# Routing tables, first-slot weights and weight loads re-ordered in an attention and mixture-of-experts kernel

## The chip, the cores and the metric

The kernel runs on one core of one Trainium2 chip. The metric is the device time of one execution in microseconds (us), the median of a few runs. All times inside an execution are counted from the start of the profiled span.

## What is computed

```python
def reference(**kw):
    attn_out = _attn_ref(q, k, v)                 # rotary attention, 4 x 8 heads, 576 x 64
    x = attn_out as rows                          # (2304, 512)
    x = _moe_ref(x, w_gate, w_val, w_out)         # sigmoid(x@wg) * (x@wv) @ wo, d_ff 1536
    return _moe2_ref(x, ...)

def _moe2_ref(x, modality_id, w_gate, modality_bias, w1, w2):   # 2304 tokens, 8 experts
    logits = x @ w_gate + modality_bias[modality_id]
    e_idx = np.argmax(logits, axis=1)
    probs = softmax(logits)
    gate_w = probs[np.arange(N), e_idx]
    for e in range(E):
        mask = e_idx == e
        h = np.maximum(x[mask] @ w1[e], 0.0)      # (512, 1024)
        out[mask] = gate_w[mask, None] * (h @ w2[e])
    return out
```

Only the last part, `_moe2_ref`, and the end of the layer ahead of it are touched here.

## The kernel before

The kernel has three stages: attention (to about 260 us), the gated layer (to about 772 us) and the experts (to the end). Every product of two fp32 operands is made of three TensorE products: each operand is a high part in fp32r and a low part (the rest), and low times low is left out.

The end of the gated layer, `Gated.last`, makes the 18 output blocks of 128 tokens (TensorE L822, then an addition on VectorE, L1115, then a store to the row table `x2_rows` in HBM, L1125, issued from the SP queue) and, beside them, the routing. The order of this stretch is set by `Plan`: it simulates the engines with given costs and, on each engine, takes the ready step with the lowest priority number. Output block tt has priority 1000 + tt, its store 999 + tt, all routing steps -2.

The routing (`Router.route`, L1294) finds each token's expert and its place in that expert's list of slots of 256 tokens. At the end it makes three tables with one matmul chain: for each half slot and row, the token, and the high and low part of its gate weight. The operands are a one-hot of the place (`A`, written into `wb` and `spare`; a part of it is made on ScalarE from `r_d`) and three products of the one-hot of the half slot (`r_B`): with the token number, and with the two gate parts `r_gw`. The products go in three groups of 8, 8 and 2 token blocks. `tables` (L1438) turns the result, `r_ptab`, into the gather indices `r_gi`, the scatter indices `r_si` and the gates.

`Experts` then works through nine full slots and the rest. Per slot: two gathers of 128 rows by index on GpSimd's queue (`e_xg`, L1530), transposes (`e_pt`, L1541), split into `e_xh` and `e_xl`; layer 1 (96 matmuls into `e_ph`, L1560, four buffers' worth of output in three buffers); Relu and split into `e_hh` (ScalarE, L1562) and `e_hl` (VectorE, L1563); layer 2 (48 matmuls into `e_py`, L1578); scaling by the gate (L1592) and a scatter (L1593). A slot's weights come in eight parts of 512 KB: four of w1, four of w2. Each part is loaded into one of six raw buffers `wr` (L1498), copied to a high part on ScalarE (`high`, L1516) and a low part on VectorE (`low`, L1520) into one of twelve weight tiles (`e_wa`, `e_wb`, `e_w`).

The first slot's four w1 parts are loaded from SP as soon as its expert is known. Three of them are split inside the plan, between routing steps; the fourth follows in `Experts.run`. Then come `keep_warm(8)`, eight fp32 matmuls of 512 columns whose result nobody reads (L1470), and the first inputs. The w2 parts of the first slot and two w1 parts of the second are loaded from ScalarE's queue, behind the first inputs; all others from SP, each four parts ahead of its split.

Of the kernel before, what the change touches and what calls it, by code (L numbers as in the profile page):

```python
# [20 lines left out]
KC = 4  # L21
# [620 lines left out]
class Gated:  # L642
# [346 lines left out]
    def last(self, prev, r, experts):  # L989
# [196 lines left out]
class Router:  # L1186
# [107 lines left out]
    def route(self, plan, start, ps_pool, area):  # L1294
# [108 lines left out]
        do("DVE", 0.09, None, tt(out=gw[:, 1], in0=su[:, 1], in1=f32(gw[:, 0]), op=ALU.subtract), "gw")  # L1403
        do("DVE", 0.67, ["pos"], tt(out=Bm, in0=bc(self.c("ioc"), 1, NTT), in1=bc(pos[:, 2], 2, NCOL), op=ALU.is_equal), "Bm")
        groups = ((0, 8), (8, 16), (16, 18))
        for g, (k, e) in enumerate(groups):
            n, s = e - k, slice(k, e)
            A, Bv = (area[4][:, 0:256], area[4][:, 256:448]) if g == 2 else (area[2 * g], area[2 * g + 1][:, 0:768])
            Bv = Bv.rearrange("p (t a c) -> p t a c", t=n, a=3)
# [13 lines left out]
            do("DVE", 0.07 + 0.034 * n, ["Bm"], tt(out=Bv[:, :, 0], in0=Bm[:, s], in1=bc(self.c("tok")[:, s], 2, NCOL), op=ALU.mult))  # L1423
            for j in range(2):
                do("DVE", 0.07 + 0.034 * n, ["gw", "Bm"], tt(out=Bv[:, :, 1 + j], in0=Bm[:, s], in1=bc(f32(gw[:, j, s]), 2, NCOL), op=ALU.mult), f"Bv{g}")

            def table(k=k, n=n, A=A, Bv=Bv):
# [6 lines left out]
            do("PE", 0.11 * n, [f"A{g}", f"Bv{g}"] + [f"table{g - 1}"] * (g > 0), table, f"table{g}")  # L1434
        ids["table"] = ids["table2"]
        plan.add("DVE", 0.1, lambda: self.tables(st["pt"]), [ids["table"]], -2)

    def tables(self, pt):  # L1438
        V = self.nc.vector
        tt = V.tensor_tensor  # L1440
        tab = self.k([128, 4, NCOL], "r_tab")
        V.tensor_scalar(out=tab[:, 0], in0=pt[:, 0:NCOL], scalar1=-1.0, scalar2=None, op0=ALU.add)
        self.gi = self.k([128, NCOL], "r_gi", I32)
        self.si = self.k([128, NCOL], "r_si", I32)
        V.tensor_scalar(out=self.gi, in0=tab[:, 0], scalar1=0.0, scalar2=None, op0=ALU.max)
        V.tensor_scalar(out=tab[:, 1], in0=tab[:, 0], scalar1=0.0, scalar2=BIG, op0=ALU.is_lt, op1=ALU.mult)
        tt(out=self.si, in0=tab[:, 0], in1=tab[:, 1], op=ALU.add)
        V.tensor_copy(tab[:, 2], pt[:, NCOL:2 * NCOL])
        tt(out=tab[:, 3], in0=pt[:, 2 * NCOL:3 * NCOL], in1=tab[:, 2], op=ALU.add)
        self.gate = tab[:, 3]  # L1450


class Experts:
    NW = 12

    def __init__(self, tc, rawpool, xs, router, w1, w2, x2d, out, ident):
        self.tc, self.nc, self.rawpool, self.xs = tc, tc.nc, rawpool, xs
# [7 lines left out]
    def keep_warm(self, n):  # L1465

        cst = self.r.cst
        ps = self.ps.tile([128, 2, SL], F32, name="e_ph", tag="e_ph", bufs=3)
        for _ in range(n):
            self.nc.tensor.matmul(ps.rearrange("p a b -> p (a b)"), self.ident, cst[:, 0:2 * SL], start=True, stop=True)  # L1470

# [6 lines left out]
                self.t(shape, name, dt, n)  # L1478

    def load_reg(self, s):  # L1480
        engines = (mybir.EngineType.SP, mybir.EngineType.Activation)[0:2 if s < 2 else 1]
        return self.nc.values_load(self.r.esi[0:1, s:s + 1], engines=engines, min_val=0, max_val=NE - 1,
                                   skip_runtime_bounds_check_because="clamped on chip")

    def load(self, s, k, dma=None):

        nc = self.nc
        if k == 0:
# [9 lines left out]
        (dma or nc.sync.dma_start)(out=dst, in_=src)  # L1498
        self.raw[s, k] = raw

    def w_tile(self):
# [45 lines left out]
    def layer1(self, s, x, between):  # L1547
# [5 lines left out]
        for f2 in range(4):  # L1553
            ps = self.ps.tile([128, 2, SL], F32, name="e_ph", tag="e_ph", bufs=3)
            for k in range(2):
                f = 2 * f2 + k
                fs = slice(128 * f, 128 * f + 128)
                mm = [(a, c, xh) for c in range(KC) for a in w[c]] + [(w[c][0], c, xl) for c in range(KC)]
                for n, (a, c, b) in enumerate(mm):
                    nc.tensor.matmul(ps[:, k], a[:, fs], b[:, c], start=n == 0, stop=n == 3 * KC - 1)  # L1560
            fs = slice(2 * f2, 2 * f2 + 2)
            nc.scalar.activation(out=hh[:, fs], in_=ps, func=AF.Relu)  # L1562
            nc.vector.scalar_tensor_tensor(out=hl[:, fs], in0=ps, scalar=0.0, in1=f32(hh[:, fs]), op0=ALU.max, op1=ALU.subtract)  # L1563
            between(f2)
        return hh, hl

# [71 lines left out]
    def run(self, pool, psum):  # L1638
# [1 line left out]
        self.pool, self.ps = pool, psum  # L1640
        self.place()
        xg = self.gather(0)
        self.split(0, KC - 1)
        self.keep_warm(8)
        x = self.inputs(0, xg)
        for k in range(KC):
            self.load(0, KC + k, nc.scalar.dma_start)
        for k in range(KC):
            self.split(0, KC + k)
            self.load(1, k, nc.scalar.dma_start if k < 2 else None)  # L1650
        for s in range(NFULL):
            last = s + 1 == NFULL

            def first(k):
                self.split(s + 1, k)
                self.load(s + 1, 4 + k)

            def second(k):
                self.split(s + 1, 4 + k)
                if not last:  # L1660
                    self.load(s + 2, k)
# [98 lines left out]
```

## Time and profile before

| | us |
|---|---|
| median of 3 runs | 1024.36 (1021.84 to 1025.43) |
| the profiled execution | 1025.67 |
| its span, first to last instruction | 1023.9 |
| TensorE busy | 987.3 (96%) |
| VectorE busy | 658.3 (64%) |
| ScalarE busy | 524.0 (51%) |
| mean granted TensorE clock | 0.994 |

The page gives, for each engine, busy time and share of the span. TensorE is busy almost throughout, and matmuls overlap, so its busy share alone does not tell how near its limit it is. The granted clock is a share of full speed: 1.0 is 2.4 GHz, 0.5 is 1.2 GHz. Of a group of overlapping instructions the timeline shows the start of the first, the time to the end of the last and their count; in brackets the idle time ahead of it and what ended it.

### The profile page before, as it was taken

Reading aid. Unit: us, or ns where it says so; the run is one execution under the profiler, and the core shown is the slowest. Engines: PE = TensorE matmul, PEld = TensorE weight load, DVE = VectorE, ACT = ScalarE, POOL = GpSimd, SP = SyncE. Lnnn points to the kernel's source line nnn. Section 1 sums busy time; section 2 is a strip of 40 time slices with the busy share of each in tenths; the row PEclk is TensorE's granted clock in tenths of the full one; section 3 lists DMA queues with packets and bytes.
Section 4 is the critical chain, followed back from the end, with each engine's and each line's share of the span. In section 5 each row is a group of like instructions: output and inputs, shape, how many; then the busy total and the mean of one; then the engine's idle time right before and its main releaser. Section 6 shows DMA issues by size and latency. Waiting matters only on the chain.

```text
span 1023.9 us, 16353 instructions
## 1 busy us (share of the span) xinstructions
PE 987.3 (96%) x6085; PEld 908.6 (89%) x6085; DVE 658.3 (64%) x1196; ACT 524.0 (51%) x1038; POOL 352.1 (34%) x272
## 2 busy tenths in 40 slices
PE   8899999998999999999999999999998899999996
PEld 7889899988989999999999999998886899999994
DVE  8999999999977746535535536422365655556651
ACT  6889899888967422222212222223313555555542
POOL 5888769565313423223313322301101021111111
PEclk9999999999999999999999999999999999999998
DMA  6897777765311302101101101000046966767640
GB/s 209 249 264 186 203 190 197 186 171 148 93 54 62 104 21 64 42 21 62 49 14 62 62 22 43 20 1 1 1 139 223 325 225 221 223 226 225 222 161 25
DMA packets 61399, 128.42 MB, mean 125 GB/s; under 512 B 6575, under 2 KB 20543, under 8 KB 61312
## 3 DMA queue, kind: packets, MB, share of 16 engines
q1 hardware_dynamic: 56896, 114.45, 37.2%
q0 software_dynamic: 3040, 9.70, 2.9%
q10 hardware_dynamic: 1376, 3.15, 0.8%
q8 instruction: 50, 0.82, 0.3%
q14 instruction: 37, 0.30, 0.1%
HBM read 95.65 MB, written 9.77 MB: 103 GB/s over the span
## 4 chain that ended last, share of the span: by engine, by line
PE 51%; issue 18%; ACT 6%; DMA 6%; DVE 6%; POOL 2%; SPq 0%; POOLq 0%; DVEq 0%; ACTq 0%
PE gv L753 29%; PE yo L822 13%; DMA out<-e_y,r_si 5%; PE pv L322 2%; ACT e L244 2%; ACT pth L305 2%; PE s L222 2%; DVE e L232 2%; DVE ptl L309 2%; PE pt L275 1%; PE gv L822 1%; POOL e_xg L1530 1%; PE r_pl L1270 1%; PE r_pt L1234 1%; ACT xv L330 1%
## 5 line engine op out<-in xcount | busy, mean ns | idle before, releaser
L762 POOL TENSOR_TENSOR gl<-sg,gh 128x384 fp32r<-128x384 f32 x60 | 63.4, 1057 | 259.5 <-ACT gh L761 259.5
L760 DVE TENSOR_TENSOR sg<-gv,sg 128x384 f32<-128x384 f32 x70 | 39.0, 557 | 142.1 <-PE gv L753 122.3
L244 ACT ACTIVATE e<-e,st 128x576 f32<-128x576 f32 x144 | 112.1, 782 | 12.7 <-DVE e L232 12.0
L759 ACT ACTIVATE sg<-gv 128x384 f32<-128x384 f32 x70 | 34.4, 491 | 145.1 <-PE gv L753 144.9
L232 DVE TENSOR_SCALAR_CACHE_REDUCE e<-s 128x576 f32<-128x576 f32 x144 | 105.3, 747 | 4.8 <-PE s L222 4.3
L309 DVE TENSOR_TENSOR ptl<-pt,pth 128x512 fp32r<-128x512 f32 x144 | 93.7, 679 | 2.8 <-ACT pth L305 1.7
L1593 POOL DMA_INDIRECT out<-e_y,r_si x19 | 19.6, 1031 | 190.3 <-ACT e_y L1592 190.3
L275 PE MATMUL pt<-cst,e 128*128 128x128 f32 x576 | 79.9, 274 | 5.1 <-DVE ptl L309 3.9
L1520 DVE TENSOR_TENSOR e_w<-wr,e_w 128x1024 fp32r<-128x1024 f32 x59 | 71.1, 1222 | 21.0 <-ACT e_w L1516 19.9
L222 PE MATMUL s<-sb 128*128 128x288 f32 x336 | 76.4, 319 | 6.4 <-DVE e L232 4.0
L761 ACT CAST gh<-sg 128x384 fp32r<-128x384 f32 x60 | 30.8, 514 | 100.4 <-DVE sg L760 100.4
L305 ACT CAST pth<-pt 128x512 fp32r<-128x512 f32 x144 | 79.3, 588 | 5.4 <-PE pt L275 4.2
L322 PE MATMUL pv<-pth,vv 128*128 128x256 f32 (+1 forms) x256 | 73.4, 309 | 6.2 <-DVE xy L340 4.6
L753 PE MATMUL gv<-xe,wb 128*128 128x384 f32 x384 | 78.9, 338 | 0.0
L275 PEld LDWEIGHTS pt<-cst,e 128*128 128x128 f32 x576 | 66.6, 141 | 9.0 <-DVE ptl L309 4.9
L753 PE MATMUL gv<-xh,wb 128*128 128x384 f32 x288 | 74.1, 338 | 0.0
L322 PE MATMUL pv<-ptl,vv 128*128 128x256 f32 (+1 forms) x256 | 69.8, 295 | 0.0
L753 PEld LDWEIGHTS gv<-xe,wb 128*128 128x128 f32 x384 | 67.1, 188 | 1.2
L1578 PE MATMUL e_py<-e_w,e_hh 128*128 128x512 f32 x216 | 67.2, 392 | 0.0
L753 PE MATMUL gv<-xh,wr 128*128 128x384 f32 x288 | 66.7, 335 | 0.0
L753 PE MATMUL gv<-xe,wr 128*128 128x384 f32 x336 | 65.0, 335 | 0.3 <-ACT xe L867 0.3
L753 PE MATMUL gv<-xl,wb 128*128 128x384 f32 x192 | 64.3, 335 | 0.0
(298 smaller groups left out, 2543.9 us busy)
## 6 DMA issues: line engine op xcount, KB each, us to landing
wr<-in_w SPq DMA_DIRECT2D x74, 512.0 KB
sb<-sa SPq DMA_DIRECT2D x60, 288.0 KB
sa<-in_qk SPq DMA_DIRECT2D x18, 576.0 KB
xy<-in_qk SPq DMA_DIRECT2D x12, 576.0 KB
wraw<-in_wg SPq DMA_DIRECT2D x12, 512.0 KB
wraw<-in_wv SPq DMA_DIRECT2D x12, 512.0 KB
wraw<-in_wo SPq DMA_DIRECT2D x12, 512.0 KB
vraw<-in_v SPq DMA_DIRECT2D x16, 320.0 KB
```

The costliest lines, as they stand in the source:

```text
L222: nc.tensor.matmul(ps[:, u, 0:SH], a, m[:, SH * u:SH * u + SH], start=n == 0, stop=n == len(mm) - 1)
L232: self.nc.vector.tensor_scalar(out=e, in0=ps[:, :, 0:SH], scalar1=-0.125, scalar2=3.0e38, op0=ALU.mult, op1=ALU.min, accum_out=st[:, 0])
L244: nc.scalar.activation(out=e, in_=e, func=AF.Exp, bias=st[:, 0], scale=-1.0, accum_out=st[:, 1])
L275: nc.tensor.transpose(pt[:, c], e[:, 128 * c:128 * c + 128], self.ident)
L305: self.nc.scalar.copy(out=hi, in_=src)
L309: self.nc.vector.tensor_tensor(out=lo, in0=src, in1=f32(hi), op=ALU.subtract)
L322: nc.tensor.matmul(ps[:, 0:w], a, m, start=n == 0, stop=n == len(mm) - 1)
L753: self.nc.tensor.matmul(p[:, 0:U], a[:, wc], b[:, c], start=c == 0 and n == 0, stop=c == KC - 1 and n == 2)
L762: (eng, {"POOL": 0.93, "DVE": 0.47}[eng], lambda: low.tensor_tensor(out=gl, in0=sg, in1=f32(gh), op=ALU.subtract))]
L822: nc.tensor.matmul(ps, a, b, start=n == 0, stop=n == 3 * len(GROUPS[grp]) - 1)
L1520: self.nc.vector.tensor_tensor(out=lo, in0=self.raw.pop((s, k)), in1=f32(hi), op=ALU.subtract)
L1578: nc.tensor.matmul(ps, a[:, f, hs], b, start=n == 0, stop=n == 23)
```

## The change

Five things are changed.

1. In the plan, routing steps that come after the token places are known (`pos`) get the priority 1017.5 instead of -2, so the output additions (1000 to 1017) go first.
2. The token table gets a matmul chain of its own, 32 columns wide, with operands `Bt`; `tables` makes only the indices. The two gate products of each group, a second chain of 64 columns (`gates`) and `gate_table` follow.
3. The first slot's w1 parts are no longer split in the plan. Their high parts stand ahead of `keep_warm`, their low parts behind the first inputs.
4. Layer 1 takes the weights' high parts first (with `e_xh`, then with `e_xl`), then the low parts. In the first slot it does so for all four `e_ph` buffers, which are now four: 64 matmuls with high parts, then 32 with low parts.
5. All loads are issued from SP, in one sequence: four, two more behind the last row store, and then one after each split, six parts ahead.

```diff
-            plan.add("DVE", 1.2, lambda k=k: experts.low(0, k), [d], 1500 + k, shared=True)
+        loads = [plan.add("SP", 0.6, lambda: experts.load_next(), [r.experts_known], 0) for k in range(KC)]
+        for k in range(2):
+            plan.add("SP", 0.6, lambda: experts.load_next(), [loads[-1], self.stored], 2000)
...
+ROUTE_LATE = 1017.5
...
+            late = "pos" in ids and prio == -2
+            i = plan.add(eng, cost + 0.08 * (eng == "DVE"), fn, d, ROUTE_LATE if late else prio, ...)
...
-            for j in range(2):
-                do("DVE", 0.07 + 0.034 * n, ["gw", "Bm"], tt(out=Bv[:, :, 1 + j], ...), f"Bv{g}")
+            do("DVE", 0.07 + 0.034 * n, ["Bm"], tt(out=Bt, in0=Bm[:, s], in1=bc(self.c("tok")[:, s], 2, NCOL), op=ALU.mult), f"Bt{g}")
...
-                    nc.tensor.matmul(st["pt"][:, 0:3 * NCOL], A[:, i], Bv[:, i].rearrange("p a c -> p (a c)"),
+                    nc.tensor.matmul(st["pt"][:, 0:NCOL], A[:, i], Bt[:, i], start=k + i == 0, stop=k + i == NTT - 1)
...
+        do("DVE", 0.5, ["table2"], lambda: self.tables(st["pt"]), "tokens")
+        for g, n, s, Bv, gates in rest:
+            for j in range(2):
+                do("DVE", 0.07 + 0.034 * n, ["gw", "tokens"], tt(out=Bv[:, :, j], ...), f"Bv{g}")
+            do("PE", 0.11 * n, [f"Bv{g}"] + [f"gates{g - 1}"] * (g > 0), gates, f"gates{g}")
+        do("DVE", 0.2, ["gates2"], lambda: self.gate_table(st["pt"]))
...
+    def load_next(self):
+        if self.loaded < 8 * (NFULL + 1):
+            self.load(*divmod(self.loaded, 8))
+            self.loaded += 1
+
+    def step(self):
+        self.split(*divmod(self.parted, 8))
+        self.parted += 1
+        self.load_next()
...
+        if parts_late:
+            for f2 in range(4):
+                products(f2, (0,))
+        for f2 in range(4):
+            products(f2, (1,) if parts_late else (0, 1))
...
-        self.split(0, KC - 1)
+        for k in range(KC):
+            self.high(0, k)
         self.keep_warm(8)
         x = self.inputs(0, xg)
         for k in range(KC):
-            self.load(0, KC + k, nc.scalar.dma_start)
-        for k in range(KC):
-            self.split(0, KC + k)
-            self.load(1, k, nc.scalar.dma_start if k < 2 else None)
+            self.low(0, k)
+            self.load_next()
+        self.parted = KC
+        for k in range(2):
+            self.step()
```

VectorE around the index tables, before (`wb` and `spare` hold the products, `r_tab` is the table being made, `y_xh` are output blocks):

```order
L1311 TENSOR_TENSOR wb<-r_B,cst 128x8x32
L1311 TENSOR_TENSOR wb<-r_B,r_gw 128x8x32 x2
L1311 TENSOR_TENSOR wb<-r_B,cst 128x8x32
L1311 TENSOR_TENSOR wb<-r_B,r_gw 128x8x32 x2
L1311 TENSOR_TENSOR spare<-r_B,cst 128x2x32
L1311 TENSOR_TENSOR spare<-r_B,r_gw 128x2x32 x2
L1115 TENSOR_TENSOR y_xh_7916<-yo,xy 128x512 x2
L1442 TENSOR_SCALAR r_tab<-r_ptab 128x32
L1445 TENSOR_SCALAR r_gi<-r_tab 128x32
L1446 TENSOR_SCALAR r_tab<-r_tab 128x32
L1447 TENSOR_TENSOR r_si<-r_tab 128x32
L1448 COPY r_tab<-r_ptab 128x32
```

and after:

```order
L1115 TENSOR_TENSOR y_xh_7911<-yo,xy 128x512
L1311 TENSOR_TENSOR r_B<-cst,r_pos 128x576
L1115 TENSOR_TENSOR y_xh_7911<-yo,xy 128x512
L1311 TENSOR_TENSOR wb<-cst,r_pos 128x1024
L1115 TENSOR_TENSOR y_xh_7911<-gv_8043,xy 128x512
L1311 TENSOR_TENSOR wb<-r_B,cst 128x256 x2
L1311 TENSOR_TENSOR spare<-r_B,cst 128x64
L1452 TENSOR_SCALAR r_tab<-r_ptab 128x32
L1455 TENSOR_SCALAR r_gi<-r_tab 128x32
L1456 TENSOR_SCALAR r_tab<-r_tab 128x32
L1457 TENSOR_TENSOR r_si<-r_tab 128x32
L1311 TENSOR_TENSOR wb<-r_B,r_gw 128x8x32 x4
```

The three output additions moved ahead of the products, and the gate products (with `r_gw`) behind the index tables.

TensorE from the last output block to layer 1 of the first slot, before:

```order
L822 MATMUL gv_8046<-wb,xl_4072 128x512 x6
L1431 MATMUL r_ptab<-wb 128x96 x16
L1431 MATMUL r_ptab<-spare 128x96 x2
L1470 MATMUL e_ph<-cst 128x512 x8
L1541 MATMUL e_pt<-cst,e_xg 128x128 x8
L1560 MATMUL e_ph<-e_xh,e_wa 128x256 x2
```

and after:

```order
L822 MATMUL gv_8043<-wb,xl_4072 128x512 x6
L1431 MATMUL r_ptab<-wb 128x32 x16
L1431 MATMUL r_ptab<-spare 128x32 x2
L1437 MATMUL r_ptab<-wb 128x64 x16
L1437 MATMUL r_ptab<-spare 128x64 x2
L1484 MATMUL e_ph<-cst 128x512 x8
L1566 MATMUL e_pt<-cst,e_xg 128x128 x8
L1592 MATMUL e_ph<-e_xh,e_wa 128x256
```

The gate chain (L1437) stands between the token chain and `keep_warm` (L1470 before, L1484 after).

VectorE from the first inputs to the first `e_hl`, before:

```order
L1520 TENSOR_TENSOR e_wb<-wr,e_wb 128x1024 x2
L1520 TENSOR_TENSOR e_w<-wr,e_w 128x1024
L1544 TENSOR_TENSOR e_xl<-e_pt,e_xh 128x4x128 x2
L1520 TENSOR_TENSOR e_w<-wr,e_w 128x1024 x4
L1563 SCALAR_TENSOR_TENSOR e_hl<-e_ph,e_hh 128x512
```

and after:

```order
L1569 TENSOR_TENSOR e_xl<-e_pt,e_xh 128x4x128 x2
L1533 TENSOR_TENSOR e_wa<-wr,e_wa 128x1024
L1533 TENSOR_TENSOR e_wb<-wr,e_wb 128x1024 x2
L1533 TENSOR_TENSOR e_w<-wr,e_w 128x1024 x3
L1601 SCALAR_TENSOR_TENSOR e_hl<-e_ph,e_hh 128x512
```

All four low parts of w1 moved behind `e_xl`, and two instead of four low parts of w2 stand ahead of the first `e_hl`.

## Rows read from the trace of the kernel before

**Rows 1.** Waits of TensorE from 740 us on: total, times, longest
```profile
PE e_ph L1560 <- DVE e_hl L1563: 3.0, 1, 3.0
PE e_pt L1541 <- DMA e_xg<-x_rows,r_gi: 1.2, 2, 0.8
PE r_ptab L1431 <- DVE wb L1311: 0.9, 1, 0.9
```

**Rows 2.** Busy time by stage, a full slot: PE, PEld, DVE, ACT, POOL, clock, DMA
```profile
828.00:851.00 23.00, 23.00 (x152) 21.11 (x151) 13.42 (x14) 12.14 (x16) 3.98 (x4) 1.00 0.69 226
```

**Rows 3.** Timeline of TensorE, 750 to 817 us and 815 to 870
```profile
771.16 1.52 PE L822 MATMUL gv<-wb,xl 128*128 128x512 f32 x6
773.63 1.09 PE L1431 MATMUL r_ptab<-wb 128*128 128x96 f32 x8 [0.94 <-DVE wb L1311]
...
776.39 0.62 PE L1431 MATMUL r_ptab<-spare 128*128 128x96 f32 x2
776.82 8.27 PE L1470 MATMUL e_ph<-cst 128*128 128x512 f32 x16
785.52 0.63 PE L1541 MATMUL e_pt<-cst,e_xg 128*128 128x128 f32 x4 [0.43 <-DMA e_xg<-x_rows,r_gi]
786.97 0.63 PE L1541 MATMUL e_pt<-cst,e_xg 128*128 128x128 f32 x4 [0.82 <-DMA e_xg<-x_rows,r_gi]
788.28 0.50 PE L1560 MATMUL e_ph<-e_xh,e_wa 128*128 128x256 f32 x2 [0.68 <-ACT e_xh L1543]
...
800.13 0.80 PE L1560 MATMUL e_ph<-e_xh,e_wa 128*128 128x256 f32 x2 [2.97 <-DVE e_hl L1563]
...
804.38 1.04 PE L1541 MATMUL e_pt<-cst,e_xg 128*128 128x128 f32 x8
805.17 0.70 PE L1578 MATMUL e_py<-e_w,e_hh 128*128 128x512 f32 x2
...
816.16 1.12 PE L1560 MATMUL e_ph<-e_xh,e_w 128*128 128x256 f32 x8
```

**Rows 4.** TensorE in slices of 1 us: length, busy (instructions), granted clock, DMA
```profile
775.00:776.00 1.00, 0.83 (x7) 0.89 0.01 4
778.00:779.00 1.00, 1.00 (x3) 0.50 0.00 0
779.00:780.00 1.00, 1.00 (x3) 0.91 0.46 174
...
802.00:803.00 1.00, 1.00 (x6) 0.50 1.04 395
```

**Rows 5.** The chain that ended last, around the first gather: start, length
```profile
778.72 2.01 DMA x_rows<-y_xh
...
781.99 1.16 POOL e_xg L1530
```

**Rows 6.** Timeline of VectorE
```profile
770.68 0.75 DVE L1311 TENSOR_TENSOR r_B<-cst,r_pos 128x576 f32<-128x576 f32 x1
771.35 1.22 DVE L1311 TENSOR_TENSOR wb<-cst,r_pos 128x1024 fp32r<-128x1024 f32 x1
772.49 0.42 DVE L1311 TENSOR_TENSOR wb<-r_B,cst 128x256 fp32r<-128x256 f32 x1
772.82 0.75 DVE L1311 TENSOR_TENSOR wb<-r_B,r_gw 128x256 fp32r<-128x256 f32 x2
...
777.28 0.18 DVE L1445 TENSOR_SCALAR r_gi<-r_tab 128x32 int32<-128x32 f32 x1
...
778.02 0.68 DVE L1115 TENSOR_TENSOR y_xh<-gv,xy 128x512 f32<-128x512 f32 x1
778.62 2.35 DVE L1520 TENSOR_TENSOR e_wb<-wr,e_wb 128x1024 fp32r<-128x1024 f32 x2
```

**Rows 7.** Timeline of ScalarE and its DMA queue (ACTq)
```profile
787.79 3.60 ACTq L1498 DMA_DIRECT2D wr<-in_w  x4
792.39 1.05 ACT L1516 CAST e_w<-wr 128x1024 fp32r<-128x1024 f32 x1 [4.17 <-DMA wr<-in_w]
...
798.12 0.59 ACT L1562 ACTIVATE e_hh<-e_ph 128x512 fp32r<-128x512 f32 x1
```

More of the change, by code (lines that the diff above doesn't have):

```diff
@@ L1304, in do @@
             d = [state["prev"]] if deps is None else [ids[x] for x in deps]
-            i = plan.add(eng, cost + 0.08 * (eng == "DVE"), fn, d, prio, shared=eng == "DVE" and deps not in (["count"], ["rank", "off"]))
+            late = "pos" in ids and prio == -2
+            i = plan.add(eng, cost + 0.08 * (eng == "DVE"), fn, d, ROUTE_LATE if late else prio, shared=eng == "DVE" and deps not in (["count"], ["rank", "off"]))
             state["prev"] = i
@@ L1405, in route @@
         groups = ((0, 8), (8, 16), (16, 18))
+        rest = []
         for g, (k, e) in enumerate(groups):
@@ L1422, in route, with table @@
                     out=A, in_=st["d"][:, k - 8:k - 8 + n], func=AF.Relu, bias=1.0, scale=-1.0), f"A{g}")
[L1423 to L1427 removed]
+            do("DVE", 0.07 + 0.034 * n, ["Bm"], tt(out=Bt, in0=Bm[:, s], in1=bc(self.c("tok")[:, s], 2, NCOL), op=ALU.mult), f"Bt{g}")
+            def table(k=k, n=n, A=A, Bt=Bt):
                 if k == 0:
@@ L1447, in tables, with gate_table @@
         tt(out=self.si, in0=tab[:, 0], in1=tab[:, 1], op=ALU.add)
-        V.tensor_copy(tab[:, 2], pt[:, NCOL:2 * NCOL])
-        tt(out=tab[:, 3], in0=pt[:, 2 * NCOL:3 * NCOL], in1=tab[:, 2], op=ALU.add)
-        self.gate = tab[:, 3]
+        self.gate, self.part = tab[:, 3], tab[:, 2]
+    def gate_table(self, pt):
+        V = self.nc.vector
+        V.tensor_copy(self.part, pt[:, NCOL:2 * NCOL])
+        V.tensor_tensor(out=self.gate, in0=pt[:, 2 * NCOL:3 * NCOL], in1=self.part, op=ALU.add)
 class Experts:
@@ L1467, in keep_warm @@
         cst = self.r.cst
-        ps = self.ps.tile([128, 2, SL], F32, name="e_ph", tag="e_ph", bufs=3)
+        ps = self.ps.tile([128, 2, SL], F32, name="e_ph", tag="e_ph", bufs=4)
         for _ in range(n):
@@ L1497, in load @@
             dst = raw.rearrange("p (a d) -> p a d", a=2)
-        (dma or nc.sync.dma_start)(out=dst, in_=src)
+        nc.sync.dma_start(out=dst, in_=src)
         self.raw[s, k] = raw
@@ L1545, in inputs, with layer1 @@
         return xh, xl
-    def layer1(self, s, x, between):
+    def layer1(self, s, x, between, parts_late=False):
         nc = self.nc
@@ L1552, in layer1, with products @@
         w = [self.w[s, c] for c in range(KC)]
-        for f2 in range(4):
-            ps = self.ps.tile([128, 2, SL], F32, name="e_ph", tag="e_ph", bufs=3)
+        ps = {}
+        def products(f2, phases):
+            if phases[0] == 0:
+                ps[f2] = self.ps.tile([128, 2, SL], F32, name="e_ph", tag="e_ph", bufs=4)
             for k in range(2):
@@ L1557, in layer1 @@
                 fs = slice(128 * f, 128 * f + 128)
-                mm = [(a, c, xh) for c in range(KC) for a in w[c]] + [(w[c][0], c, xl) for c in range(KC)]
-                for n, (a, c, b) in enumerate(mm):
-                    nc.tensor.matmul(ps[:, k], a[:, fs], b[:, c], start=n == 0, stop=n == 3 * KC - 1)
+                high = [(w[c][0], c, xh) for c in range(KC)] + [(w[c][0], c, xl) for c in range(KC)]
+                low = [(w[c][1], c, xh) for c in range(KC)]
+                for ph in phases:
+                    for n, (a, c, b) in enumerate((high, low)[ph]):
+                        nc.tensor.matmul(ps[f2][:, k], a[:, fs], b[:, c], start=k == ph == n == 0, stop=k == ph == 1 and n == KC - 1)
+        if parts_late:
[3 more added lines that the diff above has]
+            products(f2, (1,) if parts_late else (0, 1))
             fs = slice(2 * f2, 2 * f2 + 2)
-            nc.scalar.activation(out=hh[:, fs], in_=ps, func=AF.Relu)
-            nc.vector.scalar_tensor_tensor(out=hl[:, fs], in0=ps, scalar=0.0, in1=f32(hh[:, fs]), op0=ALU.max, op1=ALU.subtract)
+            nc.scalar.activation(out=hh[:, fs], in_=ps[f2], func=AF.Relu)
+            nc.vector.scalar_tensor_tensor(out=hl[:, fs], in0=ps[f2], scalar=0.0, in1=f32(hh[:, fs]), op0=ALU.max, op1=ALU.subtract)
             between(f2)
@@ L1646, in run @@
         for k in range(KC):
-            self.load(0, KC + k, nc.scalar.dma_start)
-        for k in range(KC):
-            self.split(0, KC + k)
-            self.load(1, k, nc.scalar.dma_start if k < 2 else None)
+            self.low(0, k)
[3 more added lines that the diff above has]
+            self.step()
         for s in range(NFULL):
             last = s + 1 == NFULL
[L1654 to L1661, printed above, removed]
+            next_part = lambda k: self.step()
             halves = (0,) if last else (0, 1)
             xg = self.gather(s + 1, halves)
-            hx = self.layer1(s, x, first)
+            hx = self.layer1(s, x, next_part, s == 0)
             x = self.inputs(s + 1, xg, halves)
+            if s == 0:
+                for k in range(2):
+                    self.step()
             st = {}
@@ L1669, in run @@
                     (1, 4): lambda: st.update(hx=self.half_t(st["hid"]))}
-            self.layer2(s, hx, second, also if last else None)
+            self.layer2(s, hx, next_part, also if last else None)
         self.half2(NFULL, 0, st["hx"])
```

22 lines of the change are left out of this document (11 added, 11 removed).

## Prediction

> **What bounds the kernel now.** I read three views in this order. The waits of TensorE from 740 us on come first, because TensorE is busy 96% of the span: its longest waits in the last 284 us are 3.0 us of layer 1 for VectorE, 1.2 for gathered rows and 0.9 for the table's operands [rows 1]. The stage table says where the rest of the end is decided: in a full slot TensorE is busy 23.00 of 23.00 us at full clock [rows 2]. So from the start of the first slot's layer 2 (805.17 us, first `e_py` matmul [rows 3]) to the end, nothing that comes earlier on another engine helps or hurts; the time of the kernel is that start plus a fixed rest. The question for this change is only: **when does that first `e_py` matmul start?**
>
> The timeline of TensorE gives the way there [rows 3]. The last out-product ends at 772.68 (771.16 + 1.52). The table matmuls wait 0.94 for VectorE, start at 773.63 and end at 777.01. `keep_warm` runs from 776.82 to 785.09. The transposes of the gathered rows wait 0.43, start at 785.52 and 786.97, and layer 1 starts at 788.28. At 800.13 its last two of eight output blocks start after the 2.97 us wait. Layer 2 starts at 805.17. The granted clock matters twice [rows 4]: it is 1.2 GHz (0.50) from about 775.8 to 779.2 (0.89 and 0.91 in the slices at its two ends), after TensorE had had little to do since 772.68, and again in 802 to 803 after the 2.97 us wait. Gathers start late because the last row store waits for an addition at 778.02 on VectorE, behind the tables, and lands at 780.73; the first gather then starts at 781.99 [rows 5, 6].
>
> **The change, part by part.**
>
> *Additions and stores.* Three output additions (0.69 each, about 0.61 apart) now stand before the token products; in the old order two stood before the tables and one behind them. The last waits for TensorE's 772.68. The old low part (`e_wa`, about 1.15) is gone from there. Counting on VectorE from TensorE's third-last block (two blocks of 1.36 before 772.68, so 769.97): addition 0.61, `r_B` 0.67, addition 0.61, the one-hot table 1.14, addition 0.61, first token product 0.34 plus 0.08 until it is seen [rows 6]: 774.03; with the wait for the second block about 774.17. The first table matmul starts there, 0.5 later than 773.63. The last store follows an addition that ends at 773.8 and, at the 2.01 us of the old store, lands at 775.8 instead of 780.73 [rows 5]. It is no longer what gathers wait for.
>
> *Token table.* 18 matmuls as before, but 32 columns wide instead of 96. Eight of 96 columns took 1.09, that is 0.117 each plus a tail of 0.27; those of 256 columns (eight in 1.12) go at 0.12 each [rows 3]. Width did not pay between 96 and 256, so I take 0.117 for 32 as well, and at 1.2 GHz the 0.2 of the two `spare` ones (0.62 for two with a tail of 0.41). With the clock falling at 775.8 as before, 14 go at full clock and four at half: 774.17 + 1.64 + 0.8 + 0.4 tail = 777.0; all at full clock it would be 776.5. I take 776.9. The gather indices come 0.45 later, at 777.35. That is hardly sooner than the old 777.46 [rows 6]: the gain for the gather is the store's. At the 1.26 us from release to first gather and 3.5 from there to the transposes (781.99 to 785.52 [rows 3, 5]) both halves are there by 783.6.
>
> *Gate columns.* Here is the price. The six gate products now come behind the index tables on VectorE, and `keep_warm` stands behind the 18 gate matmuls in TensorE's order. From the end of the token table: four small table operations 0.67, first pair of gate products 0.76 (two in 0.75 [rows 6]), so the gate matmuls start at 776.9 + 1.45 = 778.35. TensorE has had almost nothing to do since 772.68, a stretch more than twice as long as the one that cost the clock before, so I price them at half clock: 18 x 0.2 = 3.6, to 781.95. At full clock they would end at 780.1.
>
> The Trainium skill ("TensorE: Matmul & The Clock Gate", section "Back-to-back issue gap") has a stream of weight load and matmul pairs at about 81 ns for 128 columns at full clock. The rows here have 117 ns for 96 columns. By the page each set of 18 would be 0.65 us shorter and `keep_warm` would start 1.3 us sooner; the rows do not bear that out.
>
> *keep_warm.* The same eight matmuls. They took 8.27, of which 2.36 (776.82 to 779.2) at half clock, so 7.1 at full clock [rows 3, 4]. From 781.95 they run 7.1 plus half of whatever time the clock is still 0.50. The stretch at 0.50 before was 3.4 us long, so I take between 0 and 3.4 us of it inside `keep_warm`, and the middle, 1.7, for want of a nearer row: half of that is 0.85, and the end is at **789.9**. Before it was 785.09. The gathered rows, there at 783.6, no longer set anything: the 5 us won on the last store end in TensorE's own queue.
>
> *First inputs.* Both halves are there, so eight transposes go back to back. The second four start 0.48 after the first, and from them to layer 1 it is 1.31 as before (786.97 to 788.28): 1.79. The high parts of all four weights are done by then on ScalarE (four of 1.05 [rows 7] from about 774.5 on).
>
> *Layer 1 in two phases.* 96 matmuls at 0.12: 11.5 either way, plus 0.25 for the second half of the inputs' low part, which is wanted sooner in the new order. The low weights (four of 1.17 [rows 6], from 2.5 after `keep_warm`'s end to 7.2) are done before the low phase wants them at 9.7: moving them behind the inputs costs nothing. The 2.97 wait goes: it was there because three `e_ph` buffers were full and their emptying stood on ScalarE behind parts whose loads came late (first one at 792.39, first `e_hh` at 798.12 [rows 7]); four buffers hold the whole high phase and the loads of the first two are issued with the stores. With the wait goes the half clock at 800 to 803, which cost 1.4 (24 matmuls in 4.25 instead of 2.88). The eight transposes of the next slot add 0.79 (804.38 to 805.17).
>
> *Sum.* Layer 2 starts at 789.9 + 1.79 + 0.25 + 11.5 + 0.79 = 804.2 against 805.17: **1.0 us sooner**. From the end of `keep_warm` to layer 2 it was 20.1 and becomes 14.3, 5.8 shorter (2.97 and 1.4 in layer 1, the rest at the first inputs); 4.8 of that is given back because `keep_warm` ends later.
>
> *Loads six ahead, all from SP.* Six raw buffers, each reload held until a low part is done. The load of the first slot's seventh part is issued when the first low part is done, about 3.7 after `keep_warm`'s end (793.6), and wanted by ScalarE at 801: 7.4 us, where the first of four loads issued together took 4.6 (787.79 to 792.39 [rows 7]). In later slots VectorE is busy 13.4 of 23 us [rows 2]; no cost.
>
> **Own time.** The span is 1023.9 and the profiled execution took 1025.67, so 1.77 lies outside it. The shift makes the profiled execution 1024.7. It was itself 1.3 over the median of the three runs, 1024.36, and what counts is a median: 1024.36 - 1.0 = 1023.4.
>
> **Rivals.**
>
> *A: the clock holds.* If TensorE keeps 2.4 GHz through the tables, gate matmuls end at 780.1 and `keep_warm` at 787.2; layer 2 starts at 801.5, 3.6 sooner: 1020.8. For it: the clock is 1.00 until 775.8 although TensorE waited from 772.68. Against it: it did fall then, with less waiting than there is now. A sentence for the page beside it: the Trainium skill's 81 ns (the section named above) would shorten A by another 1.3 us, and the forecast by as much; no row here shows such a pair.
>
> *B: slower, by keep_warm.* The bound on the other side: the clock stays at 0.50 for twice the old 3.4 us after `keep_warm` starts, because the stretch ahead was so empty. From 782.1 it ends at 782.1 + 7.1 + 3.4 = 792.6, layer 2 starts at 806.95: 1.8 slower, 1026.2. It turns slower than before from an end of `keep_warm` at 790.8, only 1.0 later than forecast.
>
> *C: the wait moves into layer 2.* The first slot's last two w2 parts are made between the emptyings of layer 1. The first `e_hh` ends about 2.85 before layer 2's start and the high part behind it 1.0 later; from there three low parts (1.17) and three `e_hl` (0.6) take 5.3, so the last `e_hl` comes 3.5 after layer 2's start, and is wanted at 4.1 (six steps of three matmuls of 0.227). A load that takes 9.2 instead of 4.6 would hold this by 1.8, layer 2 by some 1.2, and leave nothing of the gain: 1024.4. Against it: six loads were in flight before, too.
>
> **How the numbers follow.** The forecast (layer 2 between 802 and 805) 0.60, A 0.17, B 0.15, C 0.08. A measurement tells 0.3%, 3.1 us, from no change; the three runs shown span 3.6. Only A reaches that far on the fast side, 0.17; of B the far end and mishaps of layer 2 do on the other, 0.06; the rest, 0.77, is the same. Range: from A's 1020.8 to B's 1026.2, with 0.2 more below for the runs' spread.
>
> **What would show it.** Right: gate matmuls (L1437) starting near 778.4 with steps of 0.2, `keep_warm` (L1484) ending at 788.5 to 791 and the first transposes right at its end with no wait for a DMA; no wait for `e_hl` in layer 1; clock 0.50 from about 776 to beyond 782, none at 800. Wrong: a DMA wait ahead of the transposes (then the gather sets the time and A or better holds), or any TensorE wait between 800 and 830.

## The result and the profile after

The changed kernel takes 1033.22 us (median of 6, 1032.21 to 1036.05) against 1023.10 for the kernel before on the same chip (6, 1021.63 to 1025.43). The ratio is 1.0089, with a 95% interval of 1.0072 to 1.0106: some 9 us slower (the two medians are 10.1 apart), where 1.0 us faster was forecast. The profiled execution took 1036.05 us with a span of 1034.1; TensorE's mean granted clock was 0.986 instead of 0.994.

The spans of the two profiles differ by 10.2 us, but 1.9 of that was there when the last out-product ended: at 774.59 (773.75 + 0.84 below) instead of 772.68 [rows 3]. That can't be put down to the change: the changed kernel and the ten made from it do the same work up to that point and end it anywhere from 770.1 to 775.7 in their profiles, on both sides of 772.68. So from here on I count from that end and call it L. From L to the end of the span it was 251.2 us and is now 259.5, **8.3 us more**.

Timeline of TensorE in the changed kernel (start, length, count; in brackets the idle time ahead and what ended it):

```profile
773.75 0.84 PE L822 MATMUL gv<-wb,xl 128*128 128x512 f32 x3
776.08 1.96 PE L1431 MATMUL r_ptab<-wb 128*128 128x32 f32 x16 [1.49 <-DVE wb L1311]
...
779.74 3.62 PE L1437 MATMUL r_ptab<-wb 128*128 128x64 f32 x16 [1.48 <-DVE wb L1311]
783.18 0.61 PE L1437 MATMUL r_ptab<-spare 128*128 128x64 f32 x2
783.60 9.98 PE L1484 MATMUL e_ph<-cst 128*128 128x512 f32 x16
793.42 1.04 PE L1566 MATMUL e_pt<-cst,e_xg 128*128 128x128 f32 x8
795.19 0.39 PE L1592 MATMUL e_ph<-e_xh,e_wa 128*128 128x256 f32 x1 [0.72 <-ACT e_xh L1568]
...
807.95 0.70 PE L1616 MATMUL e_py<-e_w,e_hh 128*128 128x512 f32 x2
...
829.97 0.64 PE L1592 MATMUL e_ph<-e_xh,e_w 128*128 128x256 f32 x4
833.69 1.04 PE L1566 MATMUL e_pt<-cst,e_xg 128*128 128x128 f32 x4 [3.09 <-DMA e_xg<-x_rows,r_gi]
836.02 1.09 PE L1566 MATMUL e_pt<-cst,e_xg 128*128 128x128 f32 x4 [1.29 <-DMA e_xg<-x_rows,r_gi]
836.76 1.20 PE L1616 MATMUL e_py<-e_wa,e_hh 128*128 128x512 f32 x2
...
861.85 0.71 PE L1616 MATMUL e_py<-e_w,e_hh 128*128 128x512 f32 x2
...
885.13 0.70 PE L1616 MATMUL e_py<-e_w,e_hh 128*128 128x512 f32 x2
```

Read the starts of layer 2, the `e_py` rows. The first slot's is at L + 33.4, against L + 32.5 before: **0.9 us late**. The next two come 28.81 and 25.09 later, where a slot takes 23.28 (861.85 to 885.13): **5.5 and 1.8 us lost**. From there on nothing is lost; together 8.2 of the 8.3.

The waits of TensorE from 740 us on (total, times, longest) and the stages, both of the changed kernel (length; busy time and count of PE, PEld, DVE, ACT, POOL; granted clock; DMA share; GB/s):

```profile
PE e_pt L1566 <- DMA e_xg<-x_rows,r_gi: 4.4, 2, 3.1
PE r_ptab L1431 <- DVE wb L1311: 1.5, 1, 1.5
PE r_ptab L1437 <- DVE wb L1311: 1.5, 1, 1.5
```

```profile
776.00:778.00 2.00, 1.92 (x17) 1.92 (x18) 0.50 (x3) 2.00 (x3) 0.00 (x0) 1.00 1.06 407
780.00:782.00 2.00, 2.00 (x11) 2.00 (x11) 0.63 (x4) 0.07 (x1) 1.17 (x1) 0.50 0.69 257
788.00:790.00 2.00, 2.00 (x5) 0.87 (x4) 0.00 (x0) 0.00 (x0) 0.00 (x0) 0.65 0.07 27
...
836.00:838.00 2.00, 1.98 (x7) 1.81 (x8) 0.31 (x2) 0.85 (x2) 0.00 (x0) 0.50 0.20 78
840.00:842.00 2.00, 2.00 (x9) 1.65 (x8) 1.07 (x1) 0.00 (x0) 0.00 (x0) 0.85 0.51 145
...
860.00:883.00 23.00, 23.00 (x152) 21.12 (x151) 13.44 (x14) 12.07 (x16) 3.99 (x4) 1.00 0.69 224
```

The 2.97 us wait for VectorE in layer 1 [rows 3] is gone, as intended. In its place TensorE waits 4.4 us for gathered rows, one slot later; the clock falls to 1.2 GHz (0.50) meanwhile and is back only after 840. The half clock stretches the transposes, which is most of the rest of the 5.5 us, and the start of the next layer 2, which is where the third slot's 1.8 us go. The full slot at 860 to 883 is what it was [rows 2].

Why the rows are late stands on POOL, which issues scatters and gathers in order. Timeline of POOL in the changed kernel, then of VectorE:

```profile
815.94 5.43 POOL L1631 DMA_INDIRECT out<-e_y,r_si  x1 [29.68 <-ACT e_y L1630]
827.57 1.00 POOL L1631 DMA_INDIRECT out<-e_y,r_si  x1 [6.20 <-DMA out<-e_y,r_si]
828.88 1.00 POOL L1555 DMA_INDIRECT e_xg<-x_rows,r_gi  x1 [0.30 <-issue]
830.18 1.23 POOL L1555 DMA_INDIRECT e_xg<-x_rows,r_gi  x1 [0.30 <-issue]
845.32 1.02 POOL L1631 DMA_INDIRECT out<-e_y,r_si  x1 [13.91 <-ACT e_y L1630]
850.76 1.00 POOL L1631 DMA_INDIRECT out<-e_y,r_si  x1 [4.42 <-ACT e_y L1630]
```

```profile
813.58 2.35 DVE L1533 TENSOR_TENSOR e_w<-wr,e_w 128x1024 fp32r<-128x1024 f32 x2
815.85 1.22 DVE L1533 TENSOR_TENSOR e_wa<-wr,e_wa 128x1024 fp32r<-128x1024 f32 x1
816.99 2.35 DVE L1533 TENSOR_TENSOR e_wb<-wr,e_wb 128x1024 fp32r<-128x1024 f32 x2
819.26 1.22 DVE L1533 TENSOR_TENSOR e_w<-wr,e_w 128x1024 fp32r<-128x1024 f32 x1
```

The first scatter takes 5.43 us on POOL, where a later one takes 1.02 (845.32), and ends at 821.37, 0.89 after VectorE's unbroken row of subtractions (820.48). The second waits 6.20 us for the first to land, and the gathers stand behind both. In the kernel before, VectorE waited 1.75 us for a cast of ScalarE at that point, and the scatter began in this gap. VectorE and POOL of the kernel before, there:

```profile
809.62 1.22 DVE L1520 TENSOR_TENSOR e_wb<-wr,e_wb 128x1024 fp32r<-128x1024 f32 x1
812.59 1.23 DVE L1520 TENSOR_TENSOR e_wb<-wr,e_wb 128x1024 fp32r<-128x1024 f32 x1 [1.75 <-ACT e_wb L1516]
```

```profile
811.89 1.02 POOL L1593 DMA_INDIRECT out<-e_y,r_si  x1 [24.97 <-ACT e_y L1592]
```

### The profile page after: what moved, and what is told of

It is laid out like the page before. It is cut to its first block, busy times and chain, and to the rows that moved or that the text cites. A ratio compares the mean times of both kernels' runs of the same rounds, so it can differ in the third digit from the quotient of the medians.

```text
span 1034.1 us, 16402 instructions
## 1 busy us (share of the span) xinstructions
PE 996.4 (96%) x6103; PEld 916.0 (89%) x6103; DVE 657.2 (64%) x1196; ACT 523.9 (51%) x1038; POOL 356.5 (34%) x272
## 4 chain that ended last, share of the span: by engine, by line
PE 53%; issue 17%; DMA 7%; DVE 5%; ACT 5%; POOL 1%; SPq 0%; POOLq 0%; ACTq 0%; DVEq 0%
PE gv L753 28%; PE yo L822 13%; DMA out<-e_y,r_si 6%; PE pv L322 3%; PE s L222 2%; PE pt L275 2%; DVE e L232 1%; ACT e L244 1%; DVE ptl L309 1%; ACT pth L305 1%; PE gv L822 1%; POOL e_xg L1555 1%; PE r_pl L1269 1%; PE r_pt L1233 1%; DVE xy L340 1%
## 5 line engine op out<-in xcount | busy, mean ns | idle before, releaser
L1631 POOL DMA_INDIRECT out<-e_y,r_si x19 | 24.0, 1264 | 196.5 <-ACT e_y L1630 190.3
L1592 PE MATMUL e_ph<-e_xh,e_w 128*128 128x256 f32 x432 | 68.4, 283 | 0.0
```

The source lines that it names most:

```text
L1592: nc.tensor.matmul(ps[f2][:, k], a[:, fs], b[:, c], start=k == ph == n == 0, stop=k == ph == 1 and n == KC - 1)
```

## The experiments

Two theories for the late rows. **P**: VectorE's subtractions, which read two operands from SBUF, keep POOL's scatter from being issued. **D**: the burst of weight loads (DMA share 0.84 to 1.04 in the six stretches of 4 us from 806 to 830) holds it up; in the kernel before the share there is 0.65 to 0.95. A third question was what `keep_warm` costs. Results at a glance, worked out from the profiles' timelines and the timed runs. "Layer 2" is the first slot's start after L, "rows" is TensorE's wait for gathered rows in the second slot. The ratio comes from all runs of a kernel, the four columns ahead of it from one execution each, and that one was the longest of 10 for steps_first (1032.07 us; median 1026.90), the shortest of 10 for warm2 (1025.46; 1028.63) and the shortest of 8 for one_phase (1029.55; 1032.77). So a few us in "L to end" are shown only where the ratio goes along:

| kernel | layer 2 | first scatter on POOL | rows | L to end | ratio to before (95%) |
|---|---|---|---|---|---|
| before | 32.5 | 1.02 | 0 | 251.2 | 1 |
| changed | 33.4 | 5.43 | 4.4 | 259.5 | 1.0089 (1.0072 to 1.0106) |
| one_input | 32.8 | 1.02 | 0.5 | 252.4 | 1.0014 (0.9986 to 1.0042) |
| half_loads | 32.8 | 5.43 | 1.9 | 254.1 | 1.0043, one run each |
| half_loads_one_input | 32.8 | 1.02 | 0 | 251.8 | 1.0029, one run each |
| steps_first | 34.5 | 4.45 | 2.4 | 257.6 | 1.0001 (0.9980 to 1.0023) |
| gather_first | 33.1 | 5.42 | 0 | 251.4 | 1.0006 (0.9984 to 1.0029) |
| warm2 | 27.7 | 2.02 | 2.7 | 251.1 | 1.0021 (1.0001 to 1.0041) |
| gather_warm1 | 26.7 | 5.42 | 0 | 245.7 | 0.9946 (0.9923 to 0.9969) |
| gather_warm0 | 28.4 | 5.43 | 0 | 246.7 | 0.9971 (0.9951 to 0.9990) |
| one_phase | 38.6 | 1.02 | 0 | 257.3 | 1.0073 (1.0051 to 1.0094) |
| gather_warm1_one_phase | 31.0 | 1.02 | 0 | 249.4 | 1.0002 (0.9982 to 1.0023) |

**one_input** changes the instruction and leaves its length:

```diff
         hi, lo = self.w[s, k]
+        if s == 1:
+            self.nc.vector.tensor_scalar(out=lo, in0=self.raw.pop((s, k)), scalar1=0.0, scalar2=3.0e38, op0=ALU.mult, op1=ALU.min,
+                                         accum_out=self.t([128, 1], "e_sum", F32, 1))
+            return
```

> The changed kernel, but the eight low parts of the second slot's weights are made by a VectorE instruction of the same shape that reads one SBUF operand (a tensor_scalar with a sum, times zero) instead of the subtraction, which reads two. These low parts are left out of the result (they are zero). Loads, casts and their order are as in the changed kernel. Theory P (the scatter's POOL instruction waits while VectorE runs subtractions with two SBUF operands back to back): the first scatter takes about 1.0 us instead of 5.43, its rows land some 4.4 us sooner, and TensorE's wait for the second slot's successor's gathered rows falls from 4.4 us to at most 1.5; time about 1027 to 1029. Theory D (the scatter waits behind the burst of weight loads on the 16 DMA engines): the first scatter still takes about 5.4 us, the wait stays about 4 us, time about 1033.

VectorE and POOL of one_input, around the first scatter:

```profile
812.04 1.22 DVE L1534 TENSOR_SCALAR_CACHE_REDUCE e_w<-wr 128x1024 fp32r<-128x1024 f32 x1
...
813.30 1.22 DVE L1534 TENSOR_SCALAR_CACHE_REDUCE e_wa<-wr 128x1024 fp32r<-128x1024 f32 x1
814.44 0.08 DVE L1534 DVE_READ_ACCUMULATOR e_wa<-wr 128x1 f32 x1
```

```profile
813.50 1.02 POOL L1635 DMA_INDIRECT out<-e_y,r_si  x1 [28.69 <-ACT e_y L1634]
820.41 1.00 POOL L1635 DMA_INDIRECT out<-e_y,r_si  x1 [5.89 <-ACT e_hh L1604]
```

VectorE is as busy as in the changed kernel, and the scatter runs through in 1.02 us, all of it inside one VectorE instruction (813.30 to 814.52), so the short gaps between them are not what let it in. With the subtractions gone and the loads left, the 5.43 is gone: P is shown for it, and D is out as its cause. (Whether it is the second operand or something else in the instruction that counts was not taken apart; and one_phase, below, shows that a row of subtractions does not always hold the scatter. Here it began 0.20 us into the instruction, in half_loads_one_input 1.09 us into one, and went through both times.) But the first scatter lands 6.1 us after its start, against 4.9 in the kernel before; the second, 0.8 behind that landing, waits 5.89 us, though its row names ScalarE; and TensorE waits 0.5 for rows. Something else is left.

The Trainium skill ("SBUF — State Buffer", section "Who interferes with whom") has a VectorE instruction with two SBUF inputs contend with a GpSimd (POOL) instruction that reads SBUF, and infers that generating DMA descriptors isn't touched by it. The first half agrees with these rows, 5.43 against 1.02 (not with one_phase, below); the second does not hold for this scatter, whose offsets lie in SBUF.

**half_loads** and **half_loads_one_input** cut the ten loads of the burst:

```diff
+        if 12 <= 8 * s + k < 22:
+            dst, src = (dst[:, 0:512], src[:, 0:512]) if k < 4 else (dst[:, 0], src[:, 0])
         nc.sync.dma_start(out=dst, in_=src)
...
+        if 12 <= 8 * s + k < 22:
+            self.raw[s, k] = bc(raw[:, 0:512], 1, 2)
```

> The changed kernel with the ten weight loads that its trace shows between 807 and 821 us cut to half their bytes (256 KB instead of 512): the second slot's four layer 2 blocks and the third slot's first six blocks use the loaded half twice, so these weights are not the reference's. Casts and subtractions keep their length and order. Theory P (VectorE's subtractions hold up the POOL instruction, and the loads only its landing): the first scatter still takes 4 to 5.5 us on POOL, but it lands 3.5 to 4.5 us after that instead of 5.4, and the gathers 2.4 to 3.5 us after theirs instead of 3.7 to 4.5; TensorE's waits for gathered rows fall from 4.4 to 0.5 to 2.5 us. Theory D (the loads hold up everything): the scatter takes about 1.0 us and no wait is left.

> half_loads and one_input together: ten loads at half their bytes (these weights use their first half twice) and the second slot's low parts made by an instruction that reads one SBUF operand (these low parts are zero). If scatter and loads are the two causes and there is no third, the scatter takes 1.0 us, lands 3.5 to 4.5 us later, the second gather's rows are there 11 to 12.5 us after the first scatter's start (15.4 in one_input, 20.0 in the changed kernel), TensorE doesn't wait for them, and from the last out-product to the end it takes 251.3 to 252.3 us. If there is a third cause, the rows come later than 14 us after the scatter's start.

POOL of half_loads, then of half_loads_one_input:

```profile
811.58 5.43 POOL L1638 DMA_INDIRECT out<-e_y,r_si  x1 [28.50 <-ACT e_y L1637]
820.78 1.00 POOL L1638 DMA_INDIRECT out<-e_y,r_si  x1 [3.78 <-DMA out<-e_y,r_si]
```

```profile
812.65 1.02 POOL L1642 DMA_INDIRECT out<-e_y,r_si  x1 [28.20 <-ACT e_y L1641]
817.76 1.00 POOL L1642 DMA_INDIRECT out<-e_y,r_si  x1 [4.09 <-DMA out<-e_y,r_si]
...
820.37 1.99 POOL L1566 DMA_INDIRECT e_xg<-x_rows,r_gi  x1 [0.30 <-issue]
```

With half the bytes the scatter's POOL time does not move (5.43), but the wait for its landing falls from 6.20 to 3.78 (it lands 3.0 us after POOL is done with it, where it was 5.4; I expected 3.5 to 4.5). So the loads are the second cause, worth some 2.4 us at that scatter. Take both away and no wait for rows is left, with 251.8 from L to the end. The second gather's rows came 13.5 us after the first scatter's start, later than the 11 to 12.5 expected and short of the 14 that would have meant a third cause; its own 1.99 us on POOL, where one takes 0.97, is 1.0 of that.

**steps_first** (two of the subtractions moved ahead of layer 1) was meant as a mild cure:

```diff
-        for k in range(2):
+        for k in range(4):
             self.step()
...
-            if s == 0:
-                for k in range(2):
-                    self.step()
```

> The changed kernel with the two steps that follow the next slot's inputs moved ahead of the first slot's layer 1, so that four steps (cast, subtraction, load) stand ahead of it and none behind the inputs. Theory P: the row of back-to-back subtractions that covers the scatter loses two (2.35 us); the scatter takes 1.0 to 3.1 us, TensorE's wait for gathered rows falls to 0 to 2.1 us; time 1026 to 1030. Theory D: as many loads are issued in the same 20 us, the scatter stays over 4 us and lands some 11 us after its start; time 1031 to 1033.

This one speaks for neither theory. The scatter took 4.45 us on POOL and landed 10.4 after its start, as D had it and beyond P's 3.1; the wait for rows, 2.4, is just beyond P's range; the time, 1026.90, is P's. Behind the scatter's start VectorE's row is 1.0 us shorter than in the changed kernel, not 2.35: it runs to 817.08, and the scatter ends 0.89 after that, at 817.97. The profile is of the longest of ten runs and has 6.4 us more than the kernel before from L to the end; as the ratio is 1.0001, most runs can't have lost that.

**gather_first** leaves the scatter late and takes the gathers out from behind it:

```diff
-            xg = self.gather(s + 1, halves)
+            if s == 0:
+                xg = self.gather(1)
             hx = self.layer1(s, x, next_part, s == 0)
             x = self.inputs(s + 1, xg, halves)
+            if not last:
+                xg = self.gather(s + 2, (0,) if s + 2 == NFULL else (0, 1))
```

> The changed kernel with each slot's gathers issued one slot sooner: behind the inputs of the slot before and ahead of that slot's two scatters on POOL, so no gather stands behind a scatter. Theories P and D alike: TensorE's 4.4 us of waits for gathered rows go, and with them the half clock behind them (836 to 841, about 1.8 us) and the stretched transposes (about 1.1); time about 1026, whatever the scatter takes. Rival (the late rows are only half of it, some later wait takes their place): over 1029.

Scatter still 5.42, TensorE never waits for rows, every slot takes 23.3: L to end 251.4, that is 8.1 of the 8.3 us back, 1026.52 us against 1025.91 for the kernel before on that chip. The ratio goes along, 1.0006 against 1.0089. The late rows were nearly all of the loss.

**warm2** has `self.keep_warm(2)`:

> The changed kernel with 2 instead of 8 keep-warm matmuls. Theory W (keep_warm is what ends last ahead of the first inputs, since the gathered rows are there by about 786): the first transposes start at about 787 instead of 793.4 (on the profile's axis), layer 2 of the first slot at 801 to 802 instead of 807.95; time 1026 to 1027. Rival (the clock needs those matmuls): the granted clock stays at 0.50 through the first inputs and part of layer 1, which gives back 2 to 5 us; time 1029 to 1032. The late scatter and TensorE's wait of about 4 us for the gathered rows stay by both.

The first transposes start at 785.21, right behind `keep_warm` (its two gathers were issued at 778.40 and 779.89), and layer 2 at L + 27.7, 4.8 us sooner than in the kernel before. The granted clock came back no later for the six matmuls fewer: it is 1.00 from 786 on (L + 13.6), in the changed kernel from 790 on (L + 15.4). The gain is then lost to late rows in the next two slots, which take 26.39 and 24.90; so the time, 1028.63, missed the 1026 to 1027 that I expected. I had also expected the scatter as late as in the changed kernel; here it got through in 2.02 us, between two subtractions, and TensorE waited 2.7 us for rows instead of about 4.

**gather_warm1** (gather_first with `keep_warm(1)`) and **gather_warm0** (without it) put the two together:

> Gathers one slot sooner, as in gather_first, and 1 keep-warm matmul instead of 8. Counted from the end of the last out-product to the end of the span: 251.4 in gather_first, 251.1 in warm2 (which loses 4.7 in its first two slots to late rows), 251.2 in the kernel before. If the two losses are separate (theory), this gives 251.4 less the 5.4 us by which warm2 begins layer 2 sooner, less about 1 for the second matmul: 244 to 246.5, and some 5 to 7 us less than the kernel before, ratio 0.993 to 0.995. Rival (an idle or short keep-warm stretch keeps the clock at 0.50 into layer 1): 247 to 250, ratio 0.996 to 0.999.

> The same with no keep-warm matmul. The second gather lands some 1.8 us after the last gate matmul, so the first transposes can't begin sooner than in gather_warm1 by more than some tenths. Theory (the clock comes back after a stretch of steady work, whatever the work is): TensorE idles about 1.8 us at 0.50, and first inputs and the start of layer 1 run at 0.50; from the last out-product to the end 244 to 248, at best equal to gather_warm1. Rival (the half clock lasts well into layer 1, 8 us of it at half): 248 to 251.

Timeline of TensorE in gather_warm1, then stages of gather_warm1 and of gather_warm0:

```profile
781.89 2.05 PE L1484 MATMUL e_ph<-cst 128*128 128x512 f32 x2
783.73 1.59 PE L1566 MATMUL e_pt<-cst,e_xg 128*128 128x128 f32 x8
786.00 0.39 PE L1592 MATMUL e_ph<-e_xh,e_wa 128*128 128x256 f32 x1 [0.68 <-ACT e_xh L1568]
```

```profile
784.00:786.00 2.00, 1.32 (x9) 1.09 (x7) 0.55 (x1) 1.17 (x3) 0.95 (x2) 0.79 0.68 211
786.00:788.00 2.00, 1.94 (x14) 1.74 (x15) 2.00 (x4) 1.85 (x2) 1.70 (x2) 1.00 0.47 154
```

```profile
788.00:790.00 2.00, 1.32 (x7) 1.06 (x6) 1.55 (x3) 1.70 (x3) 1.39 (x3) 0.50 0.64 207
792.00:794.00 2.00, 2.00 (x11) 2.00 (x11) 2.00 (x2) 0.00 (x0) 0.00 (x0) 0.50 0.81 236
```

gather_warm1 takes 1019.00 us against 1024.35 for the kernel before on that chip, ratio 0.9946 (0.9923 to 0.9969): **it beats both kernels**, by as much as expected. Without any `keep_warm` the transposes start sooner still, but the clock stays at 0.50 through the first inputs and into layer 1, and more is given back than won. The idle time that I expected there did not show; the half clock did.

**one_phase** and **gather_warm1_one_phase** take the two phases out of layer 1, in the changed kernel and in gather_warm1:

```diff
-            hx = self.layer1(s, x, next_part, s == 0)
+            hx = self.layer1(s, x, next_part)
```

> The changed kernel with the first slot's layer 1 in one phase and nothing else altered. If the crowd of subtractions behind the two-phase layer 1 is what covers the first scatter (theory P), the scatter takes 1.0 to 2.0 us here instead of 5.43 and the late rows of the next gather cost TensorE under 2 us instead of 4.4; layer 2 begins 3 to 5 us later than in the changed kernel, and from the last out-product to the end it is 257 to 261 (259.5 in the changed kernel). If the scatter waits for something else, it still takes over 4 us and the end is at 262 to 265.

> gather_warm1 with the first slot's layer 1 in one phase, as in all other slots: each of its four groups needs the low parts at once, and these come behind the inputs on VectorE, four times 1.2 us. Theory (the two phases are worth what the trace of before shows as a wait in layer 1, 3.0 us, and a little more, since the low parts now come later): TensorE waits 3 to 5 us early in layer 1, layer 2 begins 3 to 5 us later than in gather_warm1, and the steps of layer 1 are spread over its 12 us instead of its last 4, so that the first scatter takes 1.0 to 2.0 us instead of over 4. Rival (the wait drops the clock too): 5 to 8 us later.

In both the scatter takes 1.02 us and no rows are late. I expected that because layer 1's steps would be spread out; the rows do not bear this out. VectorE and POOL of one_phase, at the first scatter:

```profile
814.28 1.22 DVE L1533 TENSOR_TENSOR e_wa<-wr,e_wa 128x1024 fp32r<-128x1024 f32 x1
815.41 2.39 DVE L1533 TENSOR_TENSOR e_wb<-wr,e_wb 128x1024 fp32r<-128x1024 f32 x2
817.73 1.21 DVE L1533 TENSOR_TENSOR e_w<-wr,e_w 128x1024 fp32r<-128x1024 f32 x1
```

```profile
815.41 1.02 POOL L1631 DMA_INDIRECT out<-e_y,r_si  x1 [33.01 <-ACT e_y L1630]
```

The row of two-operand subtractions is there without a gap, to 818.94, and the scatter runs in the middle of it. So a row alone does not hold it. In both kernels with one phase the scatter began at the very time at which a subtraction began (815.41 here); in the five that took 5.42 or 5.43 us, and in warm2, it began 0.08 to 0.10 us into one, in steps_first 0.07 ahead of one. Whether this order of arrival decides was not tested, and warm2 against the five says that it is not all. What makes the two phases bring the scatter late is open.

The price of one phase is at the other end: layer 2 starts 5.2 and 4.3 us later (3 to 5 expected). The waits for low parts in layer 1 are 2.4 and 2.7 us; in one_phase the clock is also 0.50 from 794 to 800. With the gathers first, the two phases pay: 3.7 us in the profiles (249.4 less 245.7), and the ratios, 1.0002 against 0.9946, say as much or more. With the gathers behind the scatters they cost 2.2 in the profiles (259.5 less 257.3), but the intervals of the ratios, 1.0089 and 1.0073, overlap: that is not shown. Stages of one_phase:

```profile
794.00:796.00 2.00, 1.03 (x3) 0.74 (x4) 2.00 (x3) 0.00 (x0) 0.00 (x0) 0.50 0.82 290
798.00:800.00 2.00, 2.00 (x12) 2.00 (x11) 0.64 (x1) 1.27 (x2) 0.00 (x0) 0.50 0.99 389
```

## Why the prediction was wrong

- **The fixed rest: this step failed, and it is 7.4 of the 9.3 us by which the sum missed.** "Nothing that comes earlier on another engine helps or hurts" was read from TensorE being busy 23.00 of 23.00 us [rows 2]. That row says that nobody was late, not by how much. In the kernel before the gather's rows were there 11.7 us after the first scatter's start, at 823.6, and wanted at about 827.7; in the changed kernel it took 20.1 us (815.94 to 836.02), and the scatter began 1.3 us later after layer 2's start (7.99 instead of 6.72), as its `e_y` stood behind weight casts on ScalarE (it starts at 814.96 with no idle time ahead of it; in the kernel before ScalarE had waited 1.93 us for TensorE there). These 9.7 us ate the 4.1 of slack, and the rest is about the 5.5 us that the second slot lost. I named every wait between 800 and 830 as a refutation; it came at 830.6.
- **"In later slots ... no cost" for the loads and the subtractions.** True of the full slots (DMA share 0.69 in both, [rows 2]). The first slot isn't one of them: its steps are bunched, and POOL, busy 3.98 of 23.00 us in a full slot [rows 2], was the engine they hit. Rival C looked at the right crowd, but asked only whether TensorE's own operands would be late.
- **`keep_warm`: right formula, mis-sized term.** 7.1 plus half of the time at 0.50 is right: the clock stayed low to about 789.4 (0.65 in 788 to 790), 5.8 us inside `keep_warm`, and 7.1 + 2.9 is the 9.98 measured. I took 1.7 us of low clock, the middle between 0 and the old stretch. `keep_warm` ended at L + 19.0, not L + 17.2. That is past the turning point of rival B (790.8, L + 18.1), so B's mechanism held for the first layer 2: 0.9 us later than before. Some of this is chance: in the seven profiles with the same eight matmuls `keep_warm` took 8.51 (half_loads_one_input) to 9.98 us, always more than the 7.95 forecast, and in three of them layer 2 came 0.3 us later than before.
- **The steps ahead of it held.** Token matmuls at L + 1.49 as forecast, gate matmuls at L + 5.15 (5.7 forecast), at half clock, to L + 9.2 (9.3). First inputs 1.77 us (1.79), from layer 1 to layer 2 12.76 (12.5), no wait in layer 1 but the 0.7 at its start, as before. The five us won on the rows did end in TensorE's own queue, and warm2 gets them out of it (layer 2 at L + 27.7).
- **The chances.** 0.77 for no measurable difference stood on the fixed rest alone; a case "a later slot pays" was missing from the list.

## What to carry to other kernels

A full slot without waits is no proof of slack: for each transfer that feeds it, subtract landing from need, and follow its queue back to whatever it stands behind. Where gathers and scatters share POOL's in-order queue, issue the gathers first; they need nothing that the scatters make. Work that is bunched to free one engine can arrive bunched at the next, on queues that the busy shares show as idle.

## What the runs showed of the hardware

- A scatter with its offsets in SBUF, issued by POOL, took 5.43 us while VectorE ran subtractions of two SBUF operands back to back, and 1.02 under one-operand instructions of the same 1.22 us. In the changed kernel, half_loads and steps_first it ended 0.89 to 0.90 us after the last subtraction of the row, having waited for more than one of them. In warm2 (2.02) it got in at the next one, and in one_phase and gather_warm1_one_phase (1.02) it went through in the middle of such a row; what decides is open.
- 512 KB loads in a burst held a scatter's landing and not its time on POOL (5.43 either way): 6.20 us to the next scatter, 3.78 with half the bytes.
- The granted clock was back at 1.00 by L + 13.9 to 15.6 with 8 `keep_warm` matmuls (one_phase, changed kernel, gather_first), L + 13.6 with 2 (warm2), L + 14.0 with 1 (gather_warm1) and L + 20.3 with none (gather_warm0), in one profile of each; what decides it stays open.
